# A planned instruction order that reckons the denominators' transfers as longer

## The chip, the cores and the metric

The kernel runs on one core of a Trainium2 chip. The metric is the time of one execution on the device in microseconds (us). The core's engines work side by side, each through its own queue of instructions in order: PE (matrix products into PSUM), ACT (functions such as exp), DVE (elementwise work), POOL and SP. Here SP, POOL and at the start ACT issue the transfers (DMA). SBUF is the memory on the chip, PSUM the accumulators in eight banks, and DRAM holds inputs, outputs and scratch.

## What is computed

The reference applies four residual blocks to x (2048 positions, 1024 features): a linear attention with a learned feature map (A), softmax attention (B), then A and B once more with the same weights.

```python
def _B_ref(x, wqkv, wo):
    ...
    scores = jnp.einsum("bhqd,bhkd->bhqk", q, k) * (Dh ** -0.5)
    p = _softmax(scores, axis=-1)
    o = jnp.einsum("bhqk,bhkd->bhqd", p, v)
    return (lambda x, *d: x.transpose(*d))(o, 0, 2, 1, 3).reshape(B, S, D) @ wo
...
x = x + _A_ref(_layernorm(x, axis=-1), A_wqkv, A_w_phi, A_wo)
x = x + _B_ref(_layernorm(x, axis=-1), B_wqkv, B_wo)
x = x + _A_ref(_layernorm(x, axis=-1), A_wqkv, A_w_phi, A_wo)
x = x + _B_ref(_layernorm(x, axis=-1), B_wqkv, B_wo)
```

There are 32 heads of 32 features each. The softmax of B needs, for each head and query, the sum of the exponentials over all 2048 keys: the denominator.

## The kernel before, in words

The kernel does not write out its instructions directly. It first makes a list of operations (`Op`): for each, the engine or transfer queue, an estimated duration, a latency until its result may be used, the operations it needs, the memory it uses, and a priority. `Sched.run` then plays this list through on a clock of its own. On each engine it starts the ready operation with the smallest priority for which memory is free, and the order in which operations start there is the order in which the instructions are issued. So an estimate never makes the chip wait. It decides where in its engine's queue an instruction stands, and which place in memory it gets. A transfer (`dma`) is reckoned as 0.55 us of its queue and then 2.0 us plus its kilobytes / 200 until it has landed, with a further term (`ring`) for transfers that share the rings. Memory comes from one arena in SBUF and from the PSUM banks, with a quota for each class of tile (four for `T`, two each for `den` and `cden`). A tile's memory is given out again when the last operation that uses it ends on the planner's clock. On the chip a later user of that memory waits until it is really free.

Softmax attention (`attention`) goes through 32 turns in each of the two layers. A turn is one chunk of 512 queries (`qc`) with one group of four heads (`g`). In each half of a turn, PE makes scores (L1120), up to three banks at a time in alternation with three others; ACT takes their exponentials (L1136). Some tiles of scores are instead exponentiated by DVE, in steps that begin with L1050, which reads the bank, and end with L1069. PE multiplies the exponentials by the values and by a matrix of ones (L1168) into bank 6, so that rows of sums stand beside rows of outputs. DVE copies bank 6 to a tile `T` (L1184). In between PE does filler work in bank 7: keys, queries, values of coming turns, output projections, and parts of the next A block, which DVE moves out of PSUM (L935, L943, L959, L1005, L1010, and others). SP moves the keys (L927) and queries (L948, L949, and L961 to L969) to their places. A planned PE that would be too idle gets matrix products without use (L1407).

After both halves of a turn, all but the layer's last go through this chain:

1. four gathers (L1214, SP's queue) take the rows of sums out of the two `T` tiles into a small tile `cden` of 128 x 16;
2. DVE takes the reciprocals (L1219);
3. SP writes them to a scratch array `rd` in DRAM (L1220);
4. SP reads them back, each row spread over 32 partitions, into a tile `den` (L1222);
5. DVE multiplies the outputs in both `T` tiles by them (L1225, two instructions) into `oT`, which the output projection of the chunk needs later.

In the last turn of a layer there are no transfers: DVE (L1194, L1197) and ACT (L1201, L1203) do the division on the spot.

Of the kernel before, what the change touches and what calls it, by code (L numbers as in the profile page):

```python
# [25 lines left out]
class Buf:  # L26


    __slots__ = ("kind", "size", "cls", "banks", "left", "at", "with_")
# [4 lines left out]


class Op:
    __slots__ = ("eng", "dur", "lat", "fn", "bufs", "prio", "mode", "ndep", "out", "t", "start", "seq", "accum", "first", "ahead", "along", "drain", "rows")

    def __init__(self, eng, dur, lat, fn, bufs, prio, mode, seq):
        self.eng, self.dur, self.lat, self.fn, self.bufs = eng, dur, lat, fn, bufs  # L40
        self.prio, self.mode, self.seq = prio, mode, seq
        self.ndep, self.out, self.t, self.start, self.accum, self.first, self.ahead, self.along, self.drain = 0, [], 0.0, None, None, False, 0.0, False, False
        self.rows = ()


LAT = {"PE": 0.2, "ACT": 0.08, "DVE": 0.1, "POOL": 0.2, "SP": 2.0, "AQ": 2.0, "GQ": 2.5}
# [7 lines left out]
class Sched:  # L54
# [11 lines left out]
    def op(self, eng, dur, fn, deps=(), bufs=(), prio=0.0, lat=None, mode=None):  # L66
        o = Op(eng, dur, LAT[eng] if lat is None else lat, fn, tuple(bufs), prio, mode, len(self.ops))
        for d in deps:
            if d is not None:
                d.out.append(o)  # L70
                o.ndep += 1
        for b in o.bufs:
            b.left += 1
        if eng == "DVE" and any(b.kind == "ps" and b.banks in ([(7,)], [(6,)]) for b in o.bufs):
            o.ahead = EVAC
        self.ops.append(o)
        return o
# [76 lines left out]
    def run(self):  # L154
# [7 lines left out]
        mode = {e: None for e in engines}  # L162
# [3 lines left out]
        first = {}  # L166
# [11 lines left out]
        accum = False  # L178
        ring = 0.0
        rows = ()  # L180
# [5 lines left out]
        t, left, order = 0.0, len(self.ops), []  # L186
        while left:
            moved = False
            for e in engines:
                if busy[e] > t + 1e-9 or not ready[e]:  # L190
                    continue
                skipped = []
                pick = None
                full = e == "PE" and self.live.get("E", 0) >= FULL
                while ready[e] and len(skipped) < 400:
                    item = heapq.heappop(ready[e])
                    if full and not item[3].first:
                        full = False
                        held = [i for i in ready[e] if i[3].drain] if not item[3].drain else []
                        best = min(held, key=lambda i: i[:3], default=None)  # L200
                        if best is not None and self._alloc(best[3].bufs):
                            ready[e].remove(best)
                            heapq.heapify(ready[e])
                            heapq.heappush(ready[e], item)
                            pick = best[3]
                            break
                    if item[3].along and (mode[e] != item[3].mode or item[3].rows[0] in rows) and item[3].prio > now - DUE:
                        skipped.append(item)
                        continue
                    if item[3].prio <= todo[front] + WINDOW and self._alloc(item[3].bufs):  # L210
                        pick = item[3]
                        break
                    skipped.append(item)
                for s in skipped:
                    heapq.heappush(ready[e], s)
                if pick is None and e == "PE" and self.idle is not None and self.live.get("S", 0):

                    recent = [r for r in recent if r[1] > t - SPELL]
                    worked = sum(r[1] - max(r[0], t - SPELL) for r in recent)
                    if worked >= KEEP * SPELL:  # L220
                        pass
                    elif self.bank_used[7]:

                        if accum:
                            pick = Op("PE", MM, LAT["PE"], self.idle_acc, (), 0.0, "c", 0)
                            left += 1
                    elif not self.live.get("fil", 0):
                        pick = Op("PE", MM, LAT["PE"], self.idle, (Buf("ps", 0, "idle", [(7,)]),), 0.0, "c", 0)
                        pick.bufs[0].left = 1
                        self.queue["idle"] = [list(pick.bufs), 0]  # L230
                        assert self._alloc(pick.bufs)
                        left += 1
                if pick is None:
                    continue
                if pick.first:
                    now = pick.prio
                if e == "PE":
                    recent.append((t, t + pick.dur))
                    if pick.accum is not None:
                        accum = pick.accum  # L240
                d = pick.dur
                if pick.along and (mode[e] != pick.mode or pick.rows[0] in rows):
                    d += AGAIN
                if e == "PE":
                    rows = pick.rows
                if pick.mode is not None:
                    if mode[e] is not None and mode[e] != pick.mode:
                        d += SWITCH
                    mode[e] = pick.mode
                pick.start = t  # L250
                if pick.fn not in (self.idle, self.idle_acc):
                    started[pick.prio] = started.get(pick.prio, 0) + 1
                while front < len(todo) - 1 and started.get(todo[front], 0):
                    started[todo[front]] -= 1
                    front += 1
                busy[e] = t + d
                order.append(pick)
                left -= 1
                moved = True
                n += 1  # L260
                heapq.heappush(events, (t + d, n, pick, True))
                n += 1
                lat = pick.lat
                if e in ("SP", "AQ", "GQ"):
                    ring = max(ring, t + d) + (lat - LAT[e]) * RING
                    lat = LAT[e] + ring - t - d
                heapq.heappush(events, (t + d + lat, n, pick, False))
            if moved:
                continue
# [3 lines left out]
            t = events[0][0]  # L273
            while events and events[0][0] <= t + 1e-9:
                _, _, o, own = heapq.heappop(events)
# [69 lines left out]
def kernel(  # L345
# [46 lines left out]
    pick = const.tile([P, 4], F32, tag="pick")  # L392
# [9 lines left out]
    for j in range(4):  # L402
# [4 lines left out]
        out=rep[:].rearrange("p (x j) -> p x j", j=4),  # L407
# [3 lines left out]
    for a in range(1, 4):  # L411
        nc.vector.tensor_tensor(
            out=fold[:], in0=fold[:], in1=ident[:, 32 * a:32 * a + 32], op=ALU.add
# [4 lines left out]
        out=selb[:].rearrange("p (j d) -> p j d", d=32),  # L418
        in_=pick[:].unsqueeze(2).to_broadcast([P, 4, 32]),
    )  # L420
    for a in range(4):
        for j in range(4):
            c = (j + a) % 4
            nc.vector.tensor_copy(
                out=selr[32 * a:32 * a + 32, 32 * c:32 * c + 32], in_=selb[32 * a:32 * a + 32, 32 * j:32 * j + 32])
# [24 lines left out]
    def sb(cls, *dims, dt=BF16):  # L450
        n = 1
        for d in dims:
            n *= d
        b = Buf("sb", -(-n * (4 if dt == F32 else 2) // 64) * 64, cls)
        b.with_ = ()

        def v():
            ap = arena[:, b.at // 2:b.at // 2 + n * (2 if dt == F32 else 1)]
            if dt == F32:
                ap = ap.bitcast(F32)  # L460
            if len(dims) == 2:
                ap = ap.rearrange("p (a b) -> p a b", a=dims[0])
            elif len(dims) == 3:
                ap = ap.rearrange("p (a b c) -> p a b c", a=dims[0], b=dims[1])
            return ap

        return b, v
# [606 lines left out]
    def attention(base, kT, vT, q_of, gate, extra):  # L1074
# [16 lines left out]
        while units:  # L1091
# [17 lines left out]
            prio = front = max(front, when(grp[0]))  # L1109
            deps, bufs = [], []  # L1110
# [33 lines left out]
        if True:  # L1144
            for qc, g in turns:
# [45 lines left out]
                if end:  # L1191
# [24 lines left out]
                    in_=T[k][1]()[64 * (1 - k) + 32 * i:64 * (1 - k) + 32 * i + 1, :].rearrange(  # L1216
                        "r (s c) -> r s c", c=16)),
                    [T[k][2]], [c_b, T[k][0]], kb=2) for k in range(2) for i in range(2)]
                rc = op("DVE", 0.27, lambda c_v=c_v: nc.vector.reciprocal(out=c_v(), in_=c_v()), m, [c_b], prio)  # L1219
                aw = dma(prio, lambda c_v=c_v, at_d=at_d: nc.sync.dma_start(  # L1220
                    out=at_d.rearrange("h (s c) -> (h s) c", c=16), in_=c_v()), [rc], [c_b], kb=8)
                bk = dma(prio, lambda r_v=r_v, at_d=at_d: nc.sync.dma_start(  # L1222
                    out=r_v(), in_=at_d.unsqueeze(1).to_broadcast([4, 32, C512])), [aw], [d_b], kb=600)
                o_b, o_v = sb("oT", C512)
                s = [op("DVE", dve_us(512), lambda a=a, k=k, o_v=o_v, r_v=r_v, T=T: nc.vector.tensor_tensor(  # L1225
                    out=o_v()[a, :], in0=T[k][1]()[a, :], in1=r_v()[a, :], op=ALU.mult),
# [216 lines left out]
```

## Time and profile before

| | us |
|---|---|
| median of 3 runs | 2364.65 |
| lowest, highest | 2362.11, 2368.24 |
| the profiled execution | 2371.04 |
| its span, first to last instruction | 2369.3 |
| first attention layer, about | 360 to 1275 |
| the A block between the attention layers, about | 1275 to 1493 |
| second attention layer, about | 1493 to 2357 |

The stretches of the two layers are read off the exponentials of line L1136, which start at 359.5 us, pause from about 1277 to 1493, and end at about 2357.

How to read the profile: times are us from the start of the span. A row of a timeline gives the start, the busy time, engine, line, operation, what is written and read with shapes, and how many instructions are merged; in brackets stands the idle time of that engine just before, and what ended it. "arena" is all tiles of the arena, "rd" the scratch array in DRAM. SPq is SP's queue of transfers. The time shown for an issue of a transfer is SP's own; when the transfer lands shows in whoever waits for it. The granted clock is a share of PE's full speed. The mean over the span is 0.992.

### The profile page before, as it was taken

What the parts mean: (1) busy time and instruction counts of PE and PEld (TensorE: products, weight loads), DVE (VectorE), ACT (ScalarE), POOL (GpSimd) and SP (SyncE); (2) the same over time, 40 slices, a digit from 0 to 9 for tenths busy, and PEclk for the clock granted to TensorE, in tenths of its full rate; (3) what the DMA queues carried; (4) which work ended last, traced back from release to release, by engine and by line L of the source; (5) the groups of instructions that cost most, each with busy time, mean ns of one, the idle gap of its engine ahead of it and who ended that gap; (6) DMA issues with size and microseconds to landing.
All of it is one profiled execution on the core that took longest, in us unless ns stands there. A gap on an engine that the chain in (4) does not pass through costs nothing.

```text
span 2369.3 us, 68373 instructions
## 1 busy us (share of the span) xinstructions
PE 2244.7 (95%) x29899; PEld 863.2 (36%) x29964; DVE 1760.2 (74%) x2274; ACT 2049.7 (87%) x1921; POOL 186.2 (8%) x280
## 2 busy tenths in 40 slices
PE   7999999999999999999999999999999999989998
PEld 4443343333323333333333434433333333333333
DVE  7987752567678878767974786588888988878664
ACT  5436559999999999999997555899999999999998
POOL 0110000000010110112222200000000000100000
PEclk9999999999999999999999999999999999999999
DMA  9210101112231221223323100111111111211111
GB/s 206 63 46 1 32 24 32 39 43 51 58 93 38 58 58 56 80 72 95 122 65 94 55 3 16 24 34 27 30 33 29 32 29 26 63 29 34 42 37 35
DMA packets 124259, 118.76 MB, mean 50 GB/s; under 512 B 60728, under 2 KB 102712, under 8 KB 123576
## 3 DMA queue, kind: packets, MB, share of 16 engines
q1 hardware_dynamic: 105848, 60.38, 9.6%
q0 software_dynamic: 16032, 51.92, 7.7%
q8 instruction: 234, 3.83, 0.7%
q10 hardware_dynamic: 2080, 2.10, 0.3%
q14 instruction: 65, 0.53, 0.1%
HBM read 78.71 MB, written 14.14 MB: 39 GB/s over the span
## 4 chain that ended last, share of the span: by engine, by line
ACT 33%; PE 26%; issue 9%; DVE 7%; DMA 6%; SPq 1%; ACTq 0%; DVEq 0%; POOL 0%; another core or an unknown queue 0%; POOLq 0%
ACT arena L1136 31%; PE psum L490 7%; PE psum L494 7%; PE psum L1168 6%; PE psum L1120 5%; DMA arena<-rd 3%; DVE arena L1225 1%; DVE arena L1066 1%; DMA rd<-arena 1%; DMA arena<-arena 1%; DVE arena L1069 1%; ACT arena L703 1%; DVE arena L1050 1%; DVE arena L1058 0%; DVE arena L1184 0%
## 5 line engine op out<-in xcount | busy, mean ns | idle before, releaser
L1136 ACT ACTIVATE arena<-psum 128x1536 bf16<-128x1536 f32 (+1 forms) x1366 | 1724.8, 1487 | 29.9 <-PE psum L1120 15.8
L1168 PE MATMUL psum<-arena 128*32 128x512 bf16 x4096 | 628.2, 386 | 8.8 <-DVE arena L1184 6.5
L1168 PE MATMUL psum<-arena,ones_bf 128*32 128x512 bf16 x4096 | 628.3, 386 | 0.0
L494 PE MATMUL psum<-arena 128*32 128x512 bf16 (+1 forms) x9792 | 597.2, 355 | 13.2 <-DVE arena L935 4.8
L1120 PE MATMUL psum<-arena 32*128 32x512 bf16 x4096 | 541.0, 383 | 69.3 <-ACT arena L1136 60.6
L490 PE MATMUL psum<-arena 128*128 128x512 bf16 (+1 forms) x1975 | 449.0, 375 | 12.4 <-issue 4.5
L1120 PEld LDWEIGHTS <-arena 32*128 32x128 bf16 x4096 | 176.0, 91 | 596.8 <-issue 588.5
L1066 DVE SCALAR_TENSOR_TENSOR arena<-arena 128x1024 f32<-128x1024 f32 x282 | 343.8, 1219 | 3.8 <-PE psum L1168 0.6
L494 PEld LDWEIGHTS <-arena 128*32 128x32 bf16 x9792 | 221.9, 96 | 240.3 <-issue 128.7
L490 PEld LDWEIGHTS <-arena 128*128 128x128 bf16 x2032 | 190.3, 98 | 247.4 <-issue 45.6
L1050 DVE TENSOR_SCALAR arena<-psum 128x512 int32<-128x512 f32 x282 | 192.6, 687 | 110.0 <-PE psum L1120 98.9
L1168 PEld LDWEIGHTS <-arena 128*32 128x32 bf16 x4096 | 161.0, 95 | 231.3 <-issue 187.2
L1069 DVE SCALAR_TENSOR_TENSOR arena<-arena 128x1024 bf16<-128x1024 f32 x141 | 172.0, 1220 | 7.9 <-DVE arena L1066 0.4
L1168 PEld LDWEIGHTS <-ones_bf 128*32 128x32 bf16 x4096 | 158.0, 95 | 32.0 <-issue 16.7
L935 DVE CAST arena<-psum 128x512 bf16<-128x512 f32 x120 | 82.3, 686 | 97.1 <-PE psum L494 94.5
L596 POOL DMA_DIRECT2D arena<-in_B_wqkv_dram x46 | 41.5, 903 | 1322.2 <-PE psum L494 338.8
L1225 DVE TENSOR_TENSOR arena<-arena 64x512 bf16<-64x512 f32 x124 | 84.8, 684 | 61.6 <-DMA arena<-rd 55.5
L494 PE MATMUL psum<-xT,onesD 128*32 128x512 bf16 x1236 | 116.5, 385 | 1.5 <-DVE arena L1005 1.3
L703 ACT ACTIVATE arena<-psum 128x512 bf16<-128x512 f32 x80 | 43.1, 599 | 82.2 <-PE psum L490 60.6
L1184 DVE COPY arena<-psum 128x512 f32<-128x512 f32 x126 | 86.5, 686 | 29.3 <-PE psum L1168 28.4
L1061 DVE TENSOR_SCALAR arena<-arena 128x1024 int32<-128x1024 int32 x141 | 98.9, 702 | 4.4
L1058 DVE TENSOR_SCALAR arena<-arena 128x1024 int32<-128x1024 int32 x141 | 97.6, 692 | 3.3 <-PE psum L1168 0.3
(109 smaller groups left out, 1486.7 us busy)
## 6 DMA issues: line engine op xcount, KB each, us to landing
arena<-rd SPq DMA_DIRECT2D x62, 256.0 KB
arena<-in_B_wqkv_dram POOLq DMA_DIRECT2D x58, 256.0 KB, 4.1
arena<-in_B_wo_dram POOLq DMA_DIRECT2D x40, 256.0 KB, 3.9
arena<-arena SPq DMA_DIRECT2D x256, 32.0 KB
arena<-wd_k POOLq DMA_DIRECT2D x32, 256.0 KB, 4.8
arena<-in_A_wqkv_dram POOLq DMA_DIRECT2D x32, 256.0 KB, 4.2
arena<-arena SPq DMA_DIRECT2D x96, 64.0 KB
out_dram<-arena SPq DMA_DIRECT2D x32, 128.0 KB
```

The costliest lines, as they stand in the source:

```text
L490: nc.tensor.matmul(out_, lhsT=lhsT, rhs=rhs, start=start, stop=stop, skip_group_check=True)
L494: nc.tensor.matmul(out_[ks, :], lhsT=lhsT[:, ks], rhs=rhs, start=start, stop=stop, tile_position=(0, 32 * k), skip_group_check=True)
L1050: o = op("DVE", dve_us(512), lambda: nc.vector.tensor_scalar(out=y_v()[:, k, :].bitcast(I32), in0=s_v()[:, x * C512:(x + 1) * C512], scala ...
L1058: mo = op("DVE", 1024 / 1920 + 0.15, lambda: nc.vector.tensor_scalar(out=m_v().bitcast(I32), in0=y_v().bitcast(I32), scalar1=0x7FFFFF, sca ...
L1061: po = op("DVE", 1024 / 1920 + 0.15, lambda: nc.vector.tensor_scalar(out=y_v().bitcast(I32), in0=y_v().bitcast(I32), scalar1=0x7F800000, s ...
L1066: last = [op("DVE", dve_us(1024), lambda i=i, c=c: nc.vector.scalar_tensor_tensor(out=x_v(), in0=(x_v() if i else m_v()), scalar=c, in1=m_ ...
L1069: return op("DVE", dve_us(1024), lambda: nc.vector.scalar_tensor_tensor(out=e_v(), in0=x_v(), scalar=POW2_0, in1=y_v(), op0=ALU.add, op1=A ...
L1120: nc.tensor.matmul(out=s_v()[:, x * C512:(x + 1) * C512], lhsT=kT[g][1]()[r, pp, d * P:(d + 1) * P], rhs=q_of[(qc, g)][1]()[r, (pp + j // ...
L1136: ex = op("ACT", act_us(w * C512), lambda s_v=s_v, e_v=e_v, w=w: nc.scalar.activation(out=e_v(), in_=s_v()[:, 0:w * C512], func=ACT.Exp, s ...
L1168: nc.tensor.matmul(out=a_v()[col:col + 32, :], lhsT=v_v()[:, kc % 4, o:o + DH] if what == 0 else ones_bf[:], rhs=ev()[:, x * C512:(x + 1) ...
L1184: cp = op("DVE", dve_us(512), lambda t_v=t_v, a_v=a_v: nc.vector.tensor_copy(out=t_v(), in_=a_v()), [last], [a_b, t_b], prio - 4)
L1225: s = [op("DVE", dve_us(512), lambda a=a, k=k, o_v=o_v, r_v=r_v, T=T: nc.vector.tensor_tensor(out=o_v()[a, :], in0=T[k][1]()[a, :], in1=r_ ...
```

## The change

An operation gets a further number, `slack`, zero by default. For a transfer it is added to the latency after the term for the rings has been reckoned, so that it moves that transfer's landing on the planner's clock and not the landing of other transfers. The four gathers get 1.5 us, the write to DRAM 1.0 us and the read back 2.5 us. All else in the planner is as it was, the small random factors on the durations of PE and DVE among it.

```diff
 class Op:
-    __slots__ = ("eng", "dur", "lat", "fn", "bufs", "prio", "mode", "ndep", "out", "t", "start", "seq", "accum", "first", "ahead", "along", "drain", "rows")
+    __slots__ = ("eng", "dur", "lat", "fn", "bufs", "prio", "mode", "ndep", "out", "t", "start", "seq", "accum", "first", "ahead", "along", "drain", "rows", "slack")
...
         self.rows = ()
+        self.slack = 0.0
...
                 if e in ("SP", "AQ", "GQ"):
                     ring = max(ring, t + d) + (lat - LAT[e]) * RING
-                    lat = LAT[e] + ring - t - d
+                    lat = LAT[e] + ring - t - d + pick.slack
...
                     [T[k][2]], [c_b, T[k][0]], kb=2) for k in range(2) for i in range(2)]
+                for o in m:
+                    o.slack = 1.5
                 rc = op("DVE", 0.27, lambda c_v=c_v: nc.vector.reciprocal(out=c_v(), in_=c_v()), m, [c_b], prio)
                 aw = dma(prio, lambda c_v=c_v, at_d=at_d: nc.sync.dma_start(
                     out=at_d.rearrange("h (s c) -> (h s) c", c=16), in_=c_v()), [rc], [c_b], kb=8)
                 bk = dma(prio, lambda r_v=r_v, at_d=at_d: nc.sync.dma_start(
                     out=r_v(), in_=at_d.unsqueeze(1).to_broadcast([4, 32, C512])), [aw], [d_b], kb=600)
+                aw.slack, bk.slack = 1.0, 2.5
```

## The prediction

> **What bounds the kernel now.** I read the page first, then the busy time of ACT by stretches, then the list of who waited for whom, and last the timelines around the places where ACT stood still.
>
> ```profile
> span 2369.3 us, 68373 instructions
> PE 2244.7 (95%) x29899; PEld 863.2 (36%) x29964; DVE 1760.2 (74%) x2274; ACT 2049.7 (87%) x1921; POOL 186.2 (8%) x280
> ACT 33%; PE 26%; issue 9%; DVE 7%; DMA 6%; SPq 1%; ACTq 0%; DVEq 0%; POOL 0%; another core or an unknown queue 0%; POOLq 0%
> ```
>
> The third line is the chain that ended last. Its 6% for DMA would be 142 us, but that is no saving that can be had: the chain may pass through a transfer while ACT is busy beside it. So I take ACT's own idle time as the measure, by stretches (columns: stretch, length, ACT busy, granted clock, DMA share, GB/s).
>
> ```profile
> 360.00:1275.00 915.00, 897.86 (x736) 0.99 0.23 67
> 1493.00:2357.00 864.00, 849.57 (x688) 0.99 0.12 33
> 650.00:690.00 40.00, 36.47 (x30) 1.00 0.28 79
> ```
>
> The first two rows are the two attention layers. ACT, which does most of the exponentials, is idle for 915.00 - 897.86 = 17.1 us in the one and 864.00 - 849.57 = 14.4 us in the other. That is 31.6 us in all, 1.3% of the span, and nothing that the change does within attention can give back more, since the exponentials themselves are the same. The third row, a short piece of the first, holds 40.00 - 36.47 = 3.5 us of it.
>
> What makes ACT idle? Of the waits that the edited lines can touch, these are the two on DVE (engine, line, what ended the wait: us in total, times, longest):
>
> ```profile
> DVE arena L1225 <- DMA arena<-rd: 55.5, 34, 4.1
> DVE arena L1219 <- DMA arena<-arena: 25.9, 23, 2.5
> ```
>
> L1219 is the reciprocal of the denominators and waits for the four gathers; L1225 is the pair of multiplications at the end of the chain and waits for the spread-out reciprocals to come back from DRAM. Together DVE stands 81.4 us for them. DVE is only 74% busy, so that costs nothing by itself. It costs when something urgent is queued behind. Here is one such place, DVE first and ACT after it:
>
> ```profile
> 2071.92 1.23 DVE L1069 SCALAR_TENSOR_TENSOR arena<-arena 128x1024 bf16<-128x1024 f32 x1
> 2077.21 0.68 DVE L1225 TENSOR_TENSOR arena<-arena 64x512 bf16<-64x512 f32 x1 [4.07 <-DMA arena<-rd]
> 2077.82 0.68 DVE L1184 COPY arena<-psum 128x512 f32<-128x512 f32 x1
> 2078.43 0.67 DVE L1050 TENSOR_SCALAR arena<-psum 128x512 int32<-128x512 f32 x1
> 2077.98 1.94 ACT L1136 ACTIVATE arena<-psum 128x1024 bf16<-128x1024 f32 x2 [2.34 <-issue]
> 2080.27 1.45 ACT L1136 ACTIVATE arena<-psum 128x1536 bf16<-128x1536 f32 x1 [0.35 <-PE psum L1120]
> ```
>
> DVE stands 4.07 us at L1225. Behind it wait the copy of the accumulator (L1184), which frees the bank that PE adds into, and the first step of the exponentials that DVE does itself (L1050), which frees a bank of scores. PE has no room for scores, and ACT stands 2.34 us. Then comes a second cost. The next rows are pairs of 3.41 us around the six places in mid-attention where such a wait is followed by a halved clock: the stretch before, and the stretch at 0.50 (columns: PE, PEld, DVE, ACT, POOL busy with counts, then granted clock).
>
> ```profile
> 596.96:600.37 3.41, 1.06 (x18) 0.32 (x15) 2.66 (x4) 2.31 (x2) 0.88 (x1) 1.00 0.02 5
> 600.37:603.78 3.41, 3.41 (x30) 0.86 (x31) 0.00 (x0) 2.01 (x2) 0.00 (x0) 0.50 0.34 81
> 846.13:849.54 3.41, 1.43 (x18) 0.33 (x15) 2.66 (x4) 2.52 (x2) 0.88 (x1) 1.00 0.16 19
> 849.54:852.95 3.41, 3.41 (x34) 1.01 (x35) 0.69 (x1) 2.33 (x2) 0.00 (x0) 0.50 0.18 59
> 1259.14:1262.55 3.41, 1.94 (x30) 0.67 (x23) 2.14 (x4) 3.09 (x4) 0.16 (x1) 1.00 0.01 5
> 1262.55:1265.96 3.41, 3.41 (x31) 0.89 (x34) 3.28 (x5) 1.36 (x2) 3.41 (x6) 0.50 0.52 115
> 1914.50:1917.91 3.41, 2.17 (x24) 0.45 (x23) 3.32 (x6) 1.73 (x3) 0.00 (x0) 1.00 0.02 5
> 1917.91:1921.32 3.41, 3.41 (x42) 1.27 (x42) 3.07 (x5) 2.32 (x3) 0.00 (x0) 0.50 0.17 42
> 2047.62:2051.03 3.41, 2.01 (x29) 0.71 (x29) 3.28 (x6) 2.37 (x3) 0.70 (x1) 1.00 0.24 77
> 2051.03:2054.44 3.41, 3.41 (x33) 0.97 (x35) 2.35 (x4) 3.20 (x3) 0.00 (x0) 0.50 0.02 5
> 2074.93:2078.34 3.41, 0.54 (x7) 0.28 (x4) 1.13 (x2) 1.07 (x2) 0.00 (x0) 1.00 0.11 44
> 2078.34:2081.75 3.41, 3.20 (x26) 0.65 (x25) 3.28 (x6) 3.03 (x3) 0.00 (x0) 0.50 0.02 1
> sum 40.92, PE 29.39 PEld 8.39 DVE 27.86 ACT 27.35 POOL 6.04; mean PE 2.45 PEld 0.70 DVE 2.32 ACT 2.28 POOL 0.50
> ```
>
> In the stretch ahead of each drop PE was busy only 0.54 to 2.17 us of 3.41, and then it works at half speed, too slow to keep ACT fed. In these twelve stretches ACT loses 40.92 - 27.35 = 13.6 us, or 2.26 us an episode. With the 3.5 us of the piece from 650 to 690, that makes 17.1 of the 31.6 us. In that piece there is no drop; ACT waits there for the multiplication itself, as its row shows:
>
> ```profile
> 657.33 19.89 ACT L1136 ACTIVATE arena<-psum 128x1536 bf16<-128x1536 f32 x16 [1.43 <-DVE arena L1225]
> 686.25 4.62 ACT L1136 ACTIVATE arena<-psum 128x1536 bf16<-128x1536 f32 x4 [0.73 <-DVE arena L1225]
> ```
>
> The layout gave these exponentials memory that the multiplication had to free first.
>
> **The change, part by part.** No instruction is added or removed and no wait is added. The layout's clock is told that the gathers land 1.5 us later, the write to DRAM 1.0 us and the read back 2.5 us. In the queues of their consumers, the following moves.
>
> The reciprocal L1219 comes 1.5 us later in DVE's order. The waits there are 25.9 / 23 = 1.1 us in the mean and 2.5 at the longest. If each shrinks in proportion to the longest, 1.5 / 2.5 = 60% goes (15.5 us); if the shift covers all, 25.9 us.
>
> The multiplications L1225 come 1.5 + 1.0 + 2.5 = 5.0 us later, more than the longest wait of 4.1. If the transfers are issued when they are now, all 55.5 us go. But the write (L1220) and the read back (L1222) are also put later in SP's queue, by 1.5 and 2.5 us. If SP really issues them that much later, only 2.5 us of the shift is left against the read's landing, and 2.5 / 4.1 = 61% goes (33.9 us).
>
> So 49.4 to 81.4 us of the 81.4 go, 61 to 100%. I take 80%, the middle. Of ACT's 17.1 us that is 13.7 us. Something else is late next: behind the first stall, the row at 2080.27 above shows ACT waiting 0.35 us for PE's scores. For six episodes I take off 6 x 0.35 = 2.1 us. The sum is 13.7 - 2.1 = **11.6 us less**; its own bounds are 0.61 x 17.1 - 2.1 = 8.3 us and the whole 17.1 us.
>
> The rest I cost at nothing. The two tiles of sums and the denominator tile are held 5 us longer, by the layout's reckoning. In the turn above the gathers go out at 2063.30 and the last multiplication starts at 2079.13, some 16 us; with 5 more it is 21. A turn takes 915 / 32 = 28.6 us, and the next turn wants its first tile of sums after half of that. It then takes the third of four places, so no copy waits; if the arena should be full there, an exponential would be held back, which is inside the bounds below. The products are needed only when a whole chunk is projected out, as filler work in bank 7. And memory freed later on paper means that fewer exponentials are laid onto it, which removes waits like the two at 657.33 and 686.25.
>
> SP's part decides how much of this holds, so its rows (and the chain's rows for the transfers) belong here:
>
> ```profile
> 1904.99 0.33 SPq L1220 DMA_DIRECT2D rd<-arena  x1
> 1906.19 2.75 SPq L927 DMA_DIRECT2D arena<-arena  x3
> 1909.11 0.59 SPq L1222 DMA_DIRECT2D arena<-rd  x1
> 2063.30 1.14 SPq L1214 DMA_DIRECT2D arena<-arena  x2
> 2067.62 0.33 SPq L1220 DMA_DIRECT2D rd<-arena  x1
> 2072.29 0.58 SPq L1222 DMA_DIRECT2D arena<-rd  x1
> 2079.13 0.69 DVE L1225 TENSOR_TENSOR arena<-arena 64x512 bf16<-64x512 f32 x1
> ```
>
> ```profile
> 1909.11 5.09 DMA arena<-rd
> 2067.62 4.60 DMA rd<-arena
> 2072.29 4.83 DMA arena<-rd
> ```
>
> The read back takes 4.83 to 5.09 us, close to the layout's old 5.0 beside its issue, and the write took 4.60 us against an old 2.04. So the error lies in the write, and in what stands between the two: at 1906.19 three moves of keys were queued ahead of the read back and took 2.75 us.
>
> On the halved clock the Trainium skill, "TensorE: Matmul & The Clock Gate", section "Part 1: The HAM clock gate", says that the half rate comes after at least one idle window of about 3.4 us. The rows here disagree, as PE was busy for up to 2.17 of the 3.41 us; the measurement decides. By that rule the drops would not hang on these waits; this is the third rival below.
>
> **The rivals.**
>
> *The transfers slip along with their consumers.* SP's queue is in order, and key moves wait there for DVE:
>
> ```profile
> SPq L927 <- DVE arena L935: 138.3, 48, 7.7
> ```
>
> That is 138.3 / 48 = 2.9 us each time. If the write or the read back now falls behind such a group, it comes 2.75 us later for the issues alone, and the waits grow as soon as the slip is over 2.5 us, which is what the shift leaves against the read's landing. The place is the turns with key moves for the next turns. If this makes six more stalls of the kind shown, 6 x 2.26 = 13.6 us are added: 2378 us. For it speaks the row at 1906.19; against it that at 2072.29, where SP had nothing else to issue between the two, and the same shift makes room for it.
>
> *The order is dealt anew and loses elsewhere what it gains.* From the first turn on, every later choice of the layout sees other times. The 31.6 - 17.1 = 14.5 us of other idle time can fall out larger; five new stalls at 2.26 us would eat up the 11.6. The time would be 2364.65 us, as before. Against it: in mid-attention all the drops of the clock shown above follow the waits in question.
>
> *The halved clock does not hang on these waits.* Then only the stretches ahead of the drops gain. ACT is busy there 2.31 + 2.52 + 3.09 + 1.73 + 2.37 + 1.07 = 13.1 of 20.5 us and loses 7.4. With the 3.5 us that makes 10.9; 80% of it less 2.1 us is 6.6 us, or 2358 us. The six rows of PE busy speak against it.
>
> **How the numbers follow.** The profiled execution took 2371.04 us, 1.7 us more than its span, and lies 6.4 us above the median of 2364.65. By its own time the forecast is 2359.4; against the median it is 2364.65 - 11.6 = **2353 us**. About 0.3%, or 7 us, is what a measurement of this kernel can tell from no change. The forecast has a chance of 0.46, its own range is 2347.5 to 2356.5 and it counts as faster. Loss elsewhere (0.15) and the clock (0.05) count as within 0.3%; the slip has 0.34 and counts as slower. So faster 0.46, same 0.20, slower 0.34. The range goes down to 2338, where nearly all of the 31.6 us would be gone, and up to 2382, a little beyond the slip's price.
>
> **What would show it.** In the changed profile the waits of L1225 for the read back should fall from 55.5 us to under 20, those of L1219 from 25.9 to under 12. ACT's idle time in the two attention stretches should fall from 31.6 to about 20 us, and the 3.41 us pieces at half clock in mid-attention from six to one or two. If SP's read back stands behind key moves more often and L1225 still waits 50 us or more, the slip is right. If the waits are gone and ACT's idle time is not, the new order has lost it elsewhere; then the stalls should follow waits for PE or for other transfers. If the time between the layers (1275 to 1493) changes by more than a few us, the forecast is wrong at a place that it does not treat at all.

## The result, and the profile after

| | before | after |
|---|---|---|
| median of 4 runs, us | 2365.03 | 2344.10 |
| lowest to highest, us | 2362.11 to 2368.24 | 2343.24 to 2345.34 |
| profiled execution, us | 2371.04 | 2343.24 |
| its span, us | 2369.3 | 2341.3 |
| mean granted clock | 0.992 | 0.997 |

The changed kernel is faster: its time is 0.9912 of that before (95% interval 0.9894 to 0.9929), 20.9 us by the medians. The forecast was 11.6 us; the time lies inside the wide range (2338 to 2382 us), but below the forecast's own (2347.5 to 2356.5). The two profiled executions differ by 27.8 us, because the one before lies 6 us above its median. The edit moves the line numbers a little: the reciprocals are now L1222, the write L1223, the read back L1225, the multiplications L1229, the exponentials L1137.

From the list of waits of the kernel after, the two rows that stood at 55.5 and 25.9 us (us in total, times, longest):

```profile
DVE arena L1229 <- DMA arena<-rd: 3.3, 5, 1.5
DVE arena L1222 <- DMA arena<-arena: 3.9, 4, 1.8
```

Together 7.2 us are left of 81.4. From the page and from ACT's busy time by stretches, of the kernel after (stretch, length, ACT busy, granted clock):

```profile
span 2341.3 us, 68445 instructions
PE 2235.6 (95%) x29971; PEld 865.6 (37%) x30036; DVE 1758.9 (75%) x2274; ACT 2045.6 (87%) x1921; POOL 188.4 (8%) x280
```

```profile
360.00:1262.00 902.00, 896.08 (x736) 1.00 0.24 67
1262.00:1480.00 218.00, 120.64 (x206) 0.99 0.10 28
1480.00:2330.00 850.00, 847.30 (x688) 1.00 0.13 34
```

The busy times of all engines are nearly as before, the shares too. What changed is only visible stretch by stretch. ACT is idle for 902.00 - 896.08 = 5.9 us in the first attention layer (17.1 before) and 850.00 - 847.30 = 2.7 us in the second (14.4 before): 8.6 us against 31.6. The middle part has not changed: from the end of the last exponential of the first layer to the start of the first of the second it is 216.2 us, against 216.1. Of the 27.8 us, 23.0 are this idle time of ACT. By the medians it is less: the execution profiled before was slower than usual, and 20.9 us are all that there is. Of the 27.8 us, another 4.2 are shorter busy time of the same exponentials; the page before gave 1724.8 us for them, and after:

```profile
L1137 ACT ACTIVATE arena<-psum 128x1536 bf16<-128x1536 f32 (+1 forms) x1366 | 1720.6, 1520 | 8.1 <-PE psum L1121 5.2
```

The clock column of the stretches says 1.00 where it said 0.99: none of the six pieces at half clock in mid-attention is left. Here is DVE's timeline for the turn that stood for the stalls in the prediction, now at 2046 us:

```profile
2045.90 0.24 DVE L1222 RECIPROCAL arena<-arena 128x16 f32<-128x16 f32 x1
2046.07 1.18 DVE L1067 SCALAR_TENSOR_TENSOR arena<-arena 128x1024 f32<-128x1024 f32 x1
2047.38 1.23 DVE L1070 SCALAR_TENSOR_TENSOR arena<-arena 128x1024 bf16<-128x1024 f32 x1
2050.59 0.69 DVE L1185 COPY arena<-psum 128x512 f32<-128x512 f32 x1 [1.98 <-PE psum L1169]
2051.24 0.69 DVE L1051 TENSOR_SCALAR arena<-psum 128x512 int32<-128x512 f32 x1
...
2057.13 1.28 DVE L1051 TENSOR_SCALAR arena<-psum 128x512 int32<-128x512 f32 x2
2058.33 1.39 DVE L1229 TENSOR_TENSOR arena<-arena 64x512 bf16<-64x512 f32 x2
```

The copy of the accumulator and the steps that free score banks now stand ahead of the multiplications. When these come up at 2058.33, what they need has landed, and no idle time is noted before them.

### The profile page after: what moved, and what is told of

Read it like the earlier page. It is cut to its first block, busy times and chain, and to the rows that moved or that the text cites. A ratio compares the mean times of both kernels' runs of the same rounds, so it can differ in the third digit from the quotient of the medians.

```text
span 2341.3 us, 68445 instructions
## 1 busy us (share of the span) xinstructions
PE 2235.6 (95%) x29971; PEld 865.6 (37%) x30036; DVE 1758.9 (75%) x2274; ACT 2045.6 (87%) x1921; POOL 188.4 (8%) x280
## 5 line engine op out<-in xcount | busy, mean ns | idle before, releaser
L1137 ACT ACTIVATE arena<-psum 128x1536 bf16<-128x1536 f32 (+1 forms) x1366 | 1720.6, 1520 | 8.1 <-PE psum L1121 5.2
L1067 DVE SCALAR_TENSOR_TENSOR arena<-arena 128x1024 f32<-128x1024 f32 x282 | 343.0, 1216 | 3.0
L1051 DVE TENSOR_SCALAR arena<-psum 128x512 int32<-128x512 f32 x282 | 194.0, 689 | 108.5 <-PE psum L1121 97.1
L1070 DVE SCALAR_TENSOR_TENSOR arena<-arena 128x1024 bf16<-128x1024 f32 x141 | 172.2, 1221 | 8.1 <-PE psum L1169 1.2
L1185 DVE COPY arena<-psum 128x512 f32<-128x512 f32 x126 | 86.7, 688 | 55.8 <-PE psum L1169 54.9
L495 PE MATMUL psum<-xT,onesD 128*32 128x512 bf16 x1364 | 126.9, 381 | 0.5 <-DVE arena L573 0.3
L704 ACT ACTIVATE arena<-psum 128x512 bf16<-128x512 f32 x80 | 43.1, 598 | 82.1 <-PE psum L491 60.4
L1059 DVE TENSOR_SCALAR arena<-arena 128x1024 int32<-128x1024 int32 x141 | 97.7, 693 | 3.8 <-PE psum L1121 0.3
L830 ACT ACTIVATE arena<-psum 128x512 bf16<-128x512 f32 x128 | 69.7, 597 | 33.8 <-PE psum L491 31.5
```

Source lines behind the costliest of these rows:

```text
L495: nc.tensor.matmul(out_[ks, :], lhsT=lhsT[:, ks], rhs=rhs, start=start, stop=stop, tile_position=(0, 32 * k), skip_group_check=True)
L1051: o = op("DVE", dve_us(512), lambda: nc.vector.tensor_scalar(out=y_v()[:, k, :].bitcast(I32), in0=s_v()[:, x * C512:(x + 1) * C512], scala ...
L1059: mo = op("DVE", 1024 / 1920 + 0.15, lambda: nc.vector.tensor_scalar(out=m_v().bitcast(I32), in0=y_v().bitcast(I32), scalar1=0x7FFFFF, sca ...
L1067: last = [op("DVE", dve_us(1024), lambda i=i, c=c: nc.vector.scalar_tensor_tensor(out=x_v(), in0=(x_v() if i else m_v()), scalar=c, in1=m_ ...
L1070: return op("DVE", dve_us(1024), lambda: nc.vector.scalar_tensor_tensor(out=e_v(), in0=x_v(), scalar=POW2_0, in1=y_v(), op0=ALU.add, op1=A ...
L1137: ex = op("ACT", act_us(w * C512), lambda s_v=s_v, e_v=e_v, w=w: nc.scalar.activation(out=e_v(), in_=s_v()[:, 0:w * C512], func=ACT.Exp, s ...
```

## The experiments

Two theories were put against each other. **The waits**: DVE's waits for these transfers hold up copies and score banks behind them; then PE works too little, its clock halves, and ACT starves. **The new deal**: any change of the plan deals a new order, and the gain was a lucky one. Each run gives its median and its ratio to the kernel before, measured beside it on the same chip (2360.5 to 2362.5 us), with the 95% interval. All kernels are the changed kernel with the lines shown edited.

### Which of the three numbers it is

Only the gathers:

```diff
-                aw.slack, bk.slack = 1.0, 2.5
+                aw.slack, bk.slack = 0.0, 0.0
```

> Only the four gathers are reckoned 1.5 us longer; the write and the read back are reckoned as before. Theory of the waits (DVE's waits for these transfers hold up the score banks, PE falls under about two thirds busy, its clock halves, ACT starves): the wait of the reciprocals falls from 25.9 to under 8 us, the wait of the multiplications stays at 40 to 60 us, because they move along with their own transfers. ACT's idle time falls by a quarter of what the whole change took, the half-clock pieces in mid-attention stay at 4 to 6, and the time is 2354 to 2363 us. Theory of the new deal (any change of the plan deals a new order, and the gain was luck): the time lies anywhere from 2335 to 2385 us and does not follow the waits.

Measured: 2362.77 us, ratio 1.0004 (0.9993 to 1.0015). The wait of the reciprocals is down to 8.2 us, about as expected, that of the multiplications at 37.5 us, a little under what was expected. There are four pieces at half clock between 700 and 1950 us. But there is no gain at all, where I had expected some: 35.7 of the 81.4 us of waits are gone, 18.0 of them at the multiplications, and the time has not moved.

Only the write and the read back:

```diff
-                    o.slack = 1.5
+                    o.slack = 0.0
```

> The gathers are reckoned as before; only the write (1.0 us) and the read back (2.5 us) are reckoned longer. Theory of the waits: the reciprocals still wait 20 to 30 us, the multiplications 15 us or less, instead of 55.5. Most of the gain is here: 2346 to 2354 us, with at most two half-clock pieces in mid-attention. Theory of the new deal: anywhere from 2335 to 2385 us, without regard to the waits.

Measured: 2345.06 us, ratio 0.9932 (0.9916 to 0.9949). The multiplications wait 2.0 us for the read back, the reciprocals 26.1 us. This is the whole gain within the interval.

Only the read back, by 5.0 us:

```diff
-                    o.slack = 1.5
+                    o.slack = 0.0
...
-                aw.slack, bk.slack = 1.0, 2.5
+                aw.slack, bk.slack = 0.0, 5.0
```

> All 5.0 us are put on the read back alone, so that the write and the read keep their places in the transfer queue behind the gathers, and only the multiplications move, by the full 5.0 us. Theory of the waits: the multiplications wait under 5 us in all, the reciprocals still 20 to 30 us; the time is 2345 to 2352 us, like the run with write and read back reckoned longer or a little better. If the transfers slip along with their consumers where they are moved too, this run has the read back issued about 6.0 us after the last gather, as before the change (5.96 us in the mean), and not 7.7 us as after it. Theory of the new deal: anywhere from 2335 to 2385 us.

Measured: 2344.99 us, ratio 0.9933 (0.9914 to 0.9951). The reciprocals wait 21.1 us; for the read back the multiplications no longer show a wait. From the start of the last gather's issue to that of the read back's, the timeline of SP gives 6.1 us in the mean of the 62 turns, against 6.0 before the change and 7.7 after it.

Only the read back, by 2.5 us (`aw.slack, bk.slack = 0.0, 2.5`, the gathers at 0):

> Only the read back is reckoned longer, by 2.5 us, half of the 5.0 us that brought the whole gain. Theory of the waits, as it stands after the first runs (only the multiplications' wait matters, the reciprocals' does not): the multiplications wait 8 to 25 us instead of 55.5, the reciprocals 20 to 30 us, and the time is 2344 to 2354 us. Theory of the new deal: anywhere from 2335 to 2385 us.

Measured: 2342.62 us, ratio 0.9925 (0.9910 to 0.9940). From the lists of waits, first of the run with the gathers alone, then of this one:

```profile
DVE arena L1229 <- DMA arena<-rd: 37.5, 37, 3.9
DVE arena L1222 <- DMA arena<-arena: 8.2, 4, 4.7
```

```profile
DVE arena L1222 <- DMA arena<-arena: 23.4, 21, 4.1
DVE arena L1229 <- DMA arena<-rd: 2.4, 2, 1.7
```

The two rows have changed places, and the times with them: 2362.77 us where the multiplications wait, 2342.62 where the reciprocals do. So one of the three edited numbers does it, the 2.5 us on the read back. The waits of the reciprocals, a third of the 81.4 us, cost nothing that can be measured, and 2.5 us are enough for waits that reached 4.1. From the issue of the read back to the first multiplication it is 7.1 us here in the mean of the 62 turns, against 5.4 before.

### Is it the order, or the memory?

The multiplications keep their place, but on the plan their tiles are released, and their product is ready, 5.0 us later. No transfer has slack:

```diff
-                    [bk], [o_b, r_b, T[k][0]], prio)
+                    [bk], [o_b, r_b, T[k][0]], prio, lat=LAT["DVE"] + 5.0)
```

> No transfer is reckoned longer. Instead the multiplications are reckoned to end 5.0 us later for everybody but DVE itself, so that on the plan the tiles of sums, the denominators and the product are released or ready 5.0 us later, while the multiplications keep their place. If a good part of the gain comes from where memory is laid, the time falls by 5 us or more, to under 2360 us. Theory of the waits: the two waits stay at 65 to 95 us together, ACT no longer waits for a multiplication directly (3.3 us before), and the time is 2358 to 2368 us with 4 to 8 half-clock pieces in mid-attention. Theory of the new deal: anywhere from 2335 to 2385 us.

Measured: 2379.62 us, ratio 1.0076 (1.0052 to 1.0099): slower, outside what the waits (2358 to 2368 us) and the gain from memory had, and inside the wide range of the new deal. The waits are as before, 51.9 and 23.0 us, but they fell on worse places. ACT waits for no multiplication directly any more, as expected. From the timelines of DVE and ACT in this run:

```profile
1270.82 1.40 DVE L1229 TENSOR_TENSOR arena<-arena 64x512 bf16<-64x512 f32 x2 [4.86 <-DMA arena<-rd]
1275.48 1.45 ACT L1137 ACTIVATE arena<-psum 128x1536 bf16<-128x1536 f32 x1 [4.30 <-PE psum L1121]
```

A stall of the same kind, of 4.86 us, costs ACT 4.30 us here. So the later release of memory does not bring the gain by itself; a few us of it could be hidden under the scatter. In the runs that gain, the release moved together with the order, and no run moved the order alone. And the deal does matter: with waits of the same size, a new order moves the time by some 18 us.

### The new deal by itself

The same two kernels with another seed for the small random factors, first without any slack (all three numbers at 0), then with that of the change:

```diff
-TIE = 7
+TIE = 8
```

> No slack, and another seed (8 in place of 7) for the small random factors on the planner's durations, which deals the order anew without any aim. Theory of the waits: the waits stay at 60 to 110 us together, with 4 to 9 half-clock pieces in mid-attention, and the time at 2355 to 2375 us. Theory of the new deal: a seed alone moves the time by as much as the change did, 15 to 20 us, to either side.

Measured: 2358.72 us, ratio 0.9985 (0.9976 to 0.9994); waits of 41.9 and 26.7 us, three pieces at half clock in mid-attention, two of them in a row (4 to 9 were expected). The seed alone moves the time by 3.8 us, less than the 15 to 20 of the new deal.

> The whole slack of the change with the seed 8 in place of 7. Theory of the waits: the two waits stay under 15 us together, at most two half-clock pieces in mid-attention, 2338 to 2352 us, and 12 us or more under the run with the same seed and no slack. Theory of the new deal: no fixed order between the two.

Measured: 2344.78 us, ratio 0.9924 (0.9909 to 0.9940); waits of 0.7 and 8.1 us, no piece at half clock between 360 and 1260 us or 1500 and 2330 us. Under the new seed the slack still takes 13.9 us off. The kernels whose multiplications wait 37 to 56 us take 2358.7 to 2379.6 us; those in which this wait is gone, with 2.5 to 5 us of slack on the way, take 2342.6 to 2345.1 us: five kernels with five different orders. The theory of the new deal falls as the explanation of the gain, but not as a source of scatter among kernels that stall.

### Turned round, and doubled

The sign turned (gathers -1.5, write -1.0, read back -2.5):

> The slack with its sign turned: the gathers reckoned 1.5, the write 1.0 and the read back 2.5 us shorter than before. Theory of the waits: the multiplications and reciprocals stand 5.0 us earlier in DVE's queue than before, so their waits grow from 81 us to 200 to 350 us, the half-clock pieces in mid-attention from 6 to 15 or more, and the time to 2395 to 2440 us. Theory of the new deal: within 20 us of before, on either side.

Measured: 2652.80 us, ratio 1.1226 (1.1194 to 1.1257), far over what I expected. Waits, and ACT's busy time by stretches, of this run:

```profile
DVE arena L1229 <- DMA arena<-rd: 221.7, 59, 8.1
DVE arena L1222 <- DMA arena<-arena: 93.5, 46, 4.3
```

```profile
360.00:1430.00 1070.00, 910.14 (x736) 0.92 0.19 55
1646.00:2641.00 995.00, 860.66 (x689) 0.93 0.10 29
```

The waits are in the expected range, 315 us. But ACT now loses 159.9 + 134.3 = 294 us beside 315 us of waits, where before it lost 31.6 beside 81.4. The time at half clock after 360 us is 95 times 3.41 us, against ten times before and under two after. So the price of a wait is not a constant. I read it so that up to some length ACT has scores in stock; this is not shown. Nor is it shown that the waits themselves cost nearly all of the 294 us: at half clock for 324 us, PE also does the work of 162 us less (an estimate from these pieces), and no run tells the two apart.

Doubled (3.0, 2.0 and 5.0):

> Twice the slack: 3.0, 2.0 and 5.0 us. Theory of the waits: they are almost gone with the single slack already (about 10 us left of 81), and ACT's idle time between exponentials is down to 8 us, so twice as much brings nothing more: 2339 to 2348 us. If holding the tiles longer costs, the time is 2350 us or more. Theory of the new deal: anywhere from 2335 to 2385 us.

Measured: 2354.91 us, ratio 0.9970 (0.9959 to 0.9981), 10.8 us more than with the single slack by the medians and 14 by the ratios, though the multiplications wait only 3.0 us for the read back. To see which half of the doubling costs, the read back alone by 10.0 us (`aw.slack, bk.slack = 0.0, 10.0`, the gathers at 0):

> The read back alone is reckoned 10.0 us longer. The multiplications stand as late as with the doubled slack, but the gathers, the reciprocals, the write and the read back keep their places. If the doubled slack lost its 11 us because the tiles are held longer, so that weights which are to lie in their memory are loaded late, this run loses them too: 2350 to 2362 us, and the loads wait over 150 us for the multiplications, against 57 us after the change. If it lost them because the transfers themselves were issued later in their queue, this run is at 2342 to 2348 us.

Measured: 2355.66 us, ratio 0.9980 (0.9969 to 0.9991). Here the transfers keep their places (6.1 us from the last gather to the read back, against 10.9 with the doubled slack), and the loss is the same. The multiplications stand equally late in both, 20.9 us after the last gather in the mean. That speaks for their lateness as what costs, and against the slip of the transfers. By which way it costs is open. The loads wait 132.9 us for the multiplications (57.1 after the change), fewer than the 150 expected. In each of the two runs PE waits for weights at one place, and the clock halves there. PE's timeline of the doubled slack and of this run:

```profile
609.19 1.05 PE L495 MATMUL psum<-arena 128*32 128x512 bf16 x16 [3.36 <-DMA arena<-in_B_wqkv_dram]
```

```profile
701.57 1.04 PE L495 MATMUL psum<-arena 128*32 128x512 bf16 x8 [2.49 <-DMA arena<-in_B_wqkv_dram]
```

A filler product waits for weights and the scores behind it wait too. ACT loses 2.96 us at the first and 2.66 at the second, and 0.92 and 0.68 on its next tile. But it is not shown that the multiplications made these loads late: by POOL's timeline their queue had stood for other instructions of DVE (L1059 until 603.37 us in the one, L1185 until 694.24 us in the other). These places explain some 3 to 4 of the 11 us; for the rest no cause was singled out.

### Another engine

The multiplications on POOL, so that nothing of DVE's stands behind their wait; first without slack, then with that of the change:

```diff
-                s = [op("DVE", dve_us(512), lambda a=a, k=k, o_v=o_v, r_v=r_v, T=T: nc.vector.tensor_tensor(
+                s = [op("POOL", 1.0, lambda a=a, k=k, o_v=o_v, r_v=r_v, T=T: nc.gpsimd.tensor_tensor(
```

> No slack, but the two multiplications of each turn run on GpSimd (POOL) instead of DVE, so that nothing of DVE's stands behind their wait; the weight loads in POOL's queue stand there instead. Theory of the waits: DVE no longer waits for the read back at all, the half-clock pieces in mid-attention fall to two or fewer, and the time to 2338 to 2352 us, without any slack. If the gain of the change came from the later reckoning as such and not from DVE's queue, the time stays at 2355 us or more.

Measured: 2382.61 us, ratio 1.0082 (1.0052 to 1.0112).

> The multiplications on GpSimd (POOL) and the whole slack of the change. Theory of the waits: the slack has nothing left to give, since DVE waits for no read back either way; within 6 us of the run on GpSimd without slack. It is the candidate for a kernel faster than both if DVE's time matters too: 2335 to 2348 us.

Measured: 2382.40 us, ratio 1.0092 (1.0074 to 1.0110). Both miss by far, by the same amount, and neither beats the change. Beyond 2355 us, the run without slack falls where I had put the rival, a gain from the later reckoning as such. The run with slack has that reckoning and does not gain either, so the pair decides nothing between the two. DVE indeed waits for no read back any more. Without slack two new waits took its place, from the list of waits of that run:

```profile
DVE arena L1185 <- POOL arena L1229: 19.5, 11, 4.2
ACT arena L1137 <- POOL arena L1229: 14.4, 22, 1.9
```

The copy of the accumulator waits for a tile, and exponentials wait for memory, that POOL is late to free: 1.27 us a multiplication instead of 0.69, and 1.0 reckoned. With slack these two are all but gone (2.9 us for ACT), and the time is the same. ACT's idle time in attention is 42.1 us there, against 8.6 after the change, so that most of the 38 us between the two is again ACT standing still. The largest of its waits with slack, and one of PE's that is not on the list after the change:

```profile
ACT arena L1137 <- PE psum L1121: 21.2, 32, 2.1
PE psum L1121 <- DVE arena L1051: 13.0, 19, 1.7
```

PE stands for score banks that DVE frees late. The last section shows that DVE is slowed there; whether that is what makes the banks late was not taken apart.

## Why the prediction was right, and where it was not

**The bound, and the place of the gain.** ACT's idle time in attention was taken as the ceiling, 31.6 us, and the chain's 6% for DMA set aside. 23.0 us came from there, and nothing from between the layers. Of ACT's idle time 8.6 us are left, where about 20 were expected.

**The mechanism.** A wait at the multiplications, with the copy and the score banks behind it, and then the halved clock: the runs that removed this wait and left that of the reciprocals have the whole gain, and the one that lengthened both loses 290 us. PE's waits for the copy fell from 6.5 to 2.7 us, and those for L1050, 2.9 us before, are gone. But the place shown in the prediction was read wrongly in part. PE's timeline there, in the kernel before:

```profile
2075.69 0.39 PE L1120 MATMUL psum<-arena 32*128 32x512 bf16 x3 [0.62 <-ACT arena L1136]
2078.55 0.58 PE L1168 MATMUL psum<-arena 128*32 128x512 bf16 x1 [2.47 <-DVE arena L1184]
```

PE does stand for the copy. ACT, however, had scores from 2076.1 us on, and started at 2077.98, just after the first multiplication had ended (2077.21 + 0.68) and before the copy or L1050 had. So these 2.34 us look like a wait for memory that the multiplication frees, as in the rows at 657.33 and 686.25; the profile names no releaser. ACT's stall at 2048.66 us, 1.13 us at another of the six places, is put down to the multiplication itself. Waits for scores (L1120) are the largest part of ACT's idle time all the same, 15.8 of the 31.6 us; after the change they are 5.2. That no run kept the wait without the halved clock means that the clock's own share is not shown apart.

**The mis-sized term** is the first step of the sum, "80% of 17.1 us". The share of the waits that goes was taken from proportions (60 and 61% at the least); it was 91%. And of ACT's idle time more hung on the waits than the seven places that I counted: 23.0 us went by the two profiles, not 13.7. The proportion itself is not borne out: the gathers alone took 44% of the waits and no time. The deduction of 2.1 us for what is late next did not show: ACT's waits for scores fell from 22 in number to 8. The exponentials, taken as the same, were 4.2 us shorter in all: 1720.6 to 1722.3 us in the five kernels that gain, 1723.4 to 1746.1 in the five where the multiplications wait. No run shows why. That the change was worth more than the sum's own upper bound of 17.1 us was not foreseen; that the wide range held it is no merit of the sum.

**The share of the reciprocals was wrong.** I spread ACT's loss over both waits, 25.9 us of it at the reciprocals. The run with the gathers alone took 17.7 us of these away and gained nothing. The two errors, too small a share and too wide a wait, do not depend on each other.

**The slip of the transfers**, the rival on the slower side, was there in part: the read back was issued 1.7 us later behind the last gather (6.0 to 7.7 us), of the 2.5 that it needed to decide. It did not matter: from the issue of the read back to the first multiplication the change still left 8.2 us in the mean, against 5.4 before, and the 2.5 us on the read back alone, with 7.1 us, are enough.

**The new deal** as a rival of no gain fell with the second seed. Its size was not small, though: the four kernels that stall scatter over 21 us, so a single kernel with waits left would not have told much.

**The clock as a cause apart from the waits** gets no support: with the multiplications' waits gone, the half-clock pieces that followed them are gone in all five kernels; one other piece or two turn up where something else stalls, as in the run with 5.0 us on the read back (983.6 and 1075.8 us).

**Holding the tiles longer** was costed at nothing. At 5 us that holds; with the multiplications 10 us later both runs lose 11 us of the gain, and whether by held tiles or by late products is open.

## What to carry to other kernels

Where a planner writes the order, an estimate that is too short can be dearer than one that is too long (here 290 us lost at 5 us too little, 11 us of the gain at 10 us too much), for the instruction that then waits at the head of an in-order queue holds up work that was ready. Look for the wait with urgent work behind it, and move only that consumer, by some 60% of its longest wait first (here 2.5 of 4.1 us), for too much lateness has a price too. Before believing a gain of 1% from a new order, deal the order once more with another seed, with the change and without.

## What the runs showed of the hardware that was not expected

**The clock halves well before PE is idle.** In the kernel before, all drops start on the same grid of 3.41 us. Of the pieces on this grid in the profile before, from 360 us on, each one with PE busy up to 1.43 us was followed by a half-clock piece, and none with more than 2.17 us. In between both occur; these two were not followed by one (PE busy is the first entry after the length):

```profile
716.40:719.81 3.41, 1.74 (x27) 0.53 (x20) 1.84 (x3) 1.62 (x2) 0.00 (x0) 1.00 0.04 12
719.81:723.22 3.41, 3.12 (x41) 0.95 (x40) 3.38 (x6) 3.41 (x5) 0.00 (x0) 1.00 0.00 0
1173.80:1177.21 3.41, 2.15 (x33) 0.61 (x25) 3.28 (x4) 3.41 (x4) 0.00 (x0) 1.00 0.19 74
```

In the profiles of the other runs, no piece below 1.7 us went without a half-clock piece behind it, and the busiest that had one was at 2.2 us (on POOL without slack, at 1501 us). So the limit lies somewhere from 50 to 65% of a piece by the modelled times of PE, and whether a stall of 2 us costs the clock depends on how it falls on the grid. That may be why the runs before scatter over 6.1 us and those after over 2.1; no run shows it.

**POOL's work slows DVE's.** With the multiplications on POOL and the slack of the change, these groups of DVE (line, operation, count, busy us, mean ns) stand against 1216 and 692 ns after the change:

```profile
L1067 DVE SCALAR_TENSOR_TENSOR arena<-arena 128x1024 f32<-128x1024 f32 x282 | 361.6, 1282 | 2.9
L1062 DVE TENSOR_SCALAR arena<-arena 128x1024 int32<-128x1024 int32 x141 | 111.7, 792 | 4.2
L1051 DVE TENSOR_SCALAR arena<-psum 128x512 int32<-128x512 f32 x282 | 193.1, 688 | 149.9 <-PE psum L1121 137.9 <-ACT arena L1137 10.1 <-issue 0.5
```

The first two work in SBUF alone and are 66 and 100 ns longer in the mean; the third reads PSUM and is not (689 ns after the change). Where the two run side by side the cost is larger: the 29 of the 282 instructions of L1067 that overlap a multiplication take 1858 ns in the mean, the other 253 take 1216; for L1051 it is 691 and 688. In the run on POOL without slack fewer meet, and L1067 is only 5 ns longer (1221). One place, in the timelines of DVE and POOL:

```profile
2004.12 1.72 DVE L1062 TENSOR_SCALAR arena<-arena 128x1024 int32<-128x1024 int32 x1
2004.02 2.94 POOL L1229 TENSOR_TENSOR arena<-arena 64x512 bf16<-64x512 f32 x2 [21.01 <-PE psum L1169]
```

The Trainium skill, "SBUF — State Buffer", section "SBUF: two separate sides", says that GpSimd shares one pair of ports with DVE instructions that run in a mode of two ports or read two inputs from SBUF, and that the pair is held by one of them for a whole instruction, with the other blocked. The rows agree as far as they go: 1.72 us in place of 0.69 beside two operations of POOL, and no such cost for the instruction that reads PSUM.
